# One-bank score buffers for the first four tiles, a buffer of its own for the normalised rows, earlier splits, and weight loads in rows of 512 B

## The chip, the cores and the metric

The kernel runs on one core of a Trainium2 chip. A core has five engines that work side by side and wait for one another through semaphores: TensorE (PE, matmuls; PEld is its weight load), VectorE (DVE), ScalarE (ACT), GpSimd (POOL) and SyncE (SP, which here only issues transfers). Sixteen DMA engines move the data; SP's transfers go over queue q1, those that ACT issues over q10. The metric is the device time of one execution in microseconds (us).

## The reference, cut to what matters

Three stages follow each other. Attention in 4 batches of 8 heads, 576 positions and 64 numbers a head, with a mask by blocks of 64; a two-layer network on the normalised rows; and a choice of one of eight experts for each row.

```
scores = scale * np.matmul(q, k.transpose(0, 1, 3, 2))
scores = np.where(block_i >= block_j, scores, -1000000000.0)
attn = softmax(scores); attn_out = np.matmul(attn, v)          # "a"
x = attn_out.transpose(0, 2, 1, 3).reshape(B, S, H * D)
xn = (x - mu) / np.sqrt(var + 1e-06) * g_ln
x = x + np.maximum(xn @ w_ch1, 0.0) @ w_ch2                    # 512 -> 2048 -> 512
logits = x @ w_gate                                            # then one expert a row
out = p[e] * (np.maximum(x @ w1[e], 0.0) @ w2[e])
```

The inputs are of 64-bit floating point where the two weight matrices w_ch1 and w_ch2 are concerned.

## The kernel before, in words

The 2304 rows are 18 tiles of 128. Tile by tile and head by head the kernel makes scores (qk, L308), their maxima (maxes, L328), exponentials (exps, L339 to L355: exp, rounding to 16 bit, the rest by subtraction, and a transpose by DMA), and the product with v (pv, L370 and L374). Each factor is held as two 16-bit parts, so that a product is three matmuls. `finish` (L392) divides, computes mean and variance of a row (L408 and L409), normalises it (L418), splits it (L422, L423) and has it transposed (L427); L436 to L455 make the row's exact scale out of the variance. The first layer of the network (l1, L473 to L478) and the second (l2, L495 to L497, `post` from L501) work on groups of one to three tiles. `post` splits the new row (L505, L507), writes it (L509) and transposes it (L513), and `logits` (L520 to L525) multiplies it with the gate's weights.

The weights w_ch1 and w_ch2 come as 64-bit numbers, in 32 chunks of 128 x 512. `load_w` brings a chunk as 1024 words of 32 bit a partition into one of three buffers (WB = 3); 3 loads are issued on SP, 29 on ACT. `w_bits` makes 32-bit floats of it on DVE in three steps (L195, L199, L202), `w_hi` (L215, L216 on ACT) and `w_lo` (L220 on POOL) the two parts. Chunks 0 to 15 are w_ch1, 16 to 31 w_ch2; a piece of l2 can run when its four chunks are there.

A tile's k, q and v are split into two parts by `split_k`, `split_q` and `split_v` while the tile before it is at head 3 or 6; the parts of k and q lie in a ring of three buffers with the tag "nat", which the normalised rows (xh, L421) share.

The order on each engine is set when the program is built: a scheduler takes the instructions in the order of the loop from L737 and puts ready ones first by priority. `first(i)` (L720) raises the priority of attention in the first HT tiles; the conversions of weights (WPACE), and the queue of l1 and l2 pieces (L775 to L789) have none. Once built, each engine runs its list in order.

Of the kernel before, what the change touches and what calls it, by code (L numbers as in the profile page):

```python
# [10 lines left out]
F16 = mybir.dt.float16  # L11
# [57 lines left out]
ACAP = 20000  # L69
FREE = 16  # L70
HP = 400
HT = 2
MAN = 0
FS = 7
G2 = 68
# [11 lines left out]
def kernel(  # L87
# [42 lines left out]
    actx = dctx.enter_context(ExitStack())  # L130
    at = actx.enter_context(tc.tile_pool(name="at", bufs=1))
    ps_a = actx.enter_context(tc.tile_pool(name="ps_a", bufs=1, space=PSUM))
    wctx = {"c": ExitStack()}
    wctx["p"] = wctx["c"].enter_context(tc.tile_pool(name="ws", bufs=1))

# [36 lines left out]
        raw[nm, i] = t  # L172

    def load_w(p, eng):
        t = wctx["p"].tile([P, 1024], I32, tag="wraw", name="wraw", bufs=WB)
        if p < 16:
            j, kk = divmod(p, KD)
            src = w_ch1[kk * P:(kk + 1) * P, 2 * j * 512:2 * (j + 1) * 512]
        else:
            src = w_ch2[(p - 16) * P:(p - 15) * P, :]  # L180
        eng.dma_start(out=t, in_=src)
        raw["w", p] = t

    wt = {}

    def w_bits(p):
        r = raw.pop(("w", p)).rearrange("p (n t) -> p n t", t=2)
        top, low = r[:, :, 1], r[:, :, 0]  # L190
        if p < 16:
            t = w2h[:, p % 4 * 2:p % 4 * 2 + 2].rearrange("p c e -> p (c e)").bitcast(I32)
        else:
            t = wp.tile([P, 512], I32, tag=("x2h", "x2t")[p % 2], name="wt", bufs=1)
        nc.vector.tensor_scalar(  # L195
            out=t, in0=top, scalar1=3, scalar2=0x3FFFFFFF,
            op0=ALU.logical_shift_left, op1=ALU.bitwise_and,
        )
        nc.vector.scalar_tensor_tensor(  # L199
            out=t, in0=top, scalar=-0x40000000, in1=t, op0=ALU.bitwise_and, op1=ALU.bitwise_or  # L200
        )
        nc.vector.scalar_tensor_tensor(  # L202
            out=t, in0=low, scalar=29, in1=t, op0=ALU.logical_shift_right, op1=ALU.bitwise_or
        )
        wt[p] = t.bitcast(F32)

    def w_parts(p):
        if p < 16:
# [17 lines left out]

    def split_q(i, eng):
        r = raw.pop(("q", i))
        n = at.tile([P, H, 2, D], F16, tag="nat", name="qn", bufs=3)
        nc.scalar.copy(out=n[:, :, 0], in_=r)  # L230
        eng.tensor_tensor(out=n[:, :, 1], in0=r, in1=n[:, :, 0], op=ALU.subtract)
        o = (KRING + VRING + turn_q[0] % 2 * 2) * 1024
        turn_q[0] += 1
        a, b = (
            spare[:, x:x + 1024].rearrange("p (h c) -> p h c", h=H) for x in (o, o + 1024)
        )
        nc.sync.dma_start_transpose(out=a, in_=n.rearrange("p h e d -> p (h e d)"))
        nc.vector.tensor_copy(b[0:D], a[D:P])
        nc.vector.tensor_copy(b[D:P], a[0:D])
        qt[i, 0], qt[i, 1] = a, b  # L240

    def split_k(i, eng):
        r = raw.pop(("k", i))
        n = at.tile([P, H, 2, D], F16, tag="nat", name="kn", bufs=3)
        nc.scalar.copy(out=n[:, :, 0], in_=r)
        eng.tensor_tensor(out=n[:, :, 1], in0=r, in1=n[:, :, 0], op=ALU.subtract)
        nc.sync.dma_start_transpose(
            out=kt[:, i % KRING], in_=n.rearrange("p h e d -> p (h e d)")
        )
# [36 lines left out]
    def qk(i, h):  # L286
        ks = keys(i)
        nk = len(ks)
        lo, n = span(i)
        m = pack(i)  # L290
        if h % m == 0:
            sps[i] = ps_a.tile([P, 1024], F32, tag="s", name="ps_s", bufs=2)
        sp = sps[i][:, h % m * n:]
        for part in range(2):
            for a, b in runs(i):
                o = lo if a == 0 else 0
                kk = ks[a] % KRING
                x, z = h % 4, h // 4
                if ks[a] % 9 == 4:
                    rhs = kt[:, kk].rearrange("p (x t) (z f s) -> p x z f t s", t=2, z=2, f=2)  # L300
                    rhs = rhs[:, x, z, 1] if o else rhs[:, x, z]
                else:
                    rhs = kt[:, kk:kk + b - a].rearrange(
                        "p n (x t) (z s) -> p x z n t s", t=2, z=2
                    )[:, x, z]
                    if b == a + 1:
                        rhs = rhs[:, 0]
                nc.tensor.matmul(  # L308
                    sp[:, a * P + o:b * P],
                    lhsT=qt[i, part].rearrange("p (x t) c -> p x (t c)", t=2)[:, x, z::2],  # L310
                    rhs=rhs,
                    start=part == 0 and a % 4 == 0,
                    stop=part == 1 and (b == 4 or b == nk),
                )
        sps[i, h] = sp
# [76 lines left out]
    def finish(i):  # L392
        sv = sums.pop(i)
        r = at.tile([P, H], F32, tag="rinv", name="rinv", bufs=2)
        nc.vector.tensor_scalar(
            out=r, in0=sv[:, 1], scalar1=P_S * 1e-9, scalar2=V_S, op0=ALU.add, op1=ALU.mult
        )
        nc.vector.reciprocal(out=r, in_=r)
        ob = obs.pop(i)
        x = wp.tile([P, H, D], F32, tag="x", name="x", bufs=6)  # L400
        nc.gpsimd.tensor_tensor(
            out=x, in0=ob, in1=r[:, :, None].to_broadcast([P, H, D]), op=ALU.mult
        )
        x = x.rearrange("p h d -> p (h d)")
        xt[i] = x
        sm = at.tile([P, 12], F32, tag="lns", name="lns", bufs=2)
        mean, var, y, w = (sm[:, c:c + 1] for c in (6, 7, 8, 9))
        nc.vector.bn_stats(out=sm[:, 0:6], in_=x)  # L408
        nc.vector.bn_aggr(out=sm[:, 6:8], in_=sm[:, 0:6])  # L409
        nc.vector.tensor_scalar(out=var, in0=var, scalar1=LN_EPS, scalar2=None, op0=ALU.add)  # L410


        nc.vector.tensor_scalar(
            out=y.bitcast(I32), in0=var.bitcast(I32), scalar1=-0.5, scalar2=1597463007.0,
            op0=ALU.mult, op1=ALU.add,
        )
        xn = at.tile([P, DM], F32, tag="ob", name="xn", bufs=2)
        nc.vector.tensor_scalar(  # L418
            out=xn, in0=x, scalar1=mean, scalar2=y, op0=ALU.subtract, op1=ALU.mult
        )  # L420
        xh = at.tile([P, 2, DM], F16, tag="nat", name="xh", bufs=3)  # L421
        nc.scalar.copy(out=xh[:, 0], in_=xn)  # L422
        nc.gpsimd.tensor_tensor(out=xh[:, 1], in0=xn, in1=xh[:, 0], op=ALU.subtract)  # L423
        g, j, n = group_of(i)
        if j == 0:
            xg[g] = wp.tile([P, 2 * KD, n * P], F16, tag="xg", name="xg", bufs=2)
        nc.sync.dma_start_transpose(  # L427
            out=xg[g][:, :, j * P:(j + 1) * P], in_=xh.rearrange("p e d -> p (e d)")
        )
        if i in GROUPS[-1]:  # L430
            c = GROUPS[-1].index(i)
            nc.vector.tensor_copy(stats[:, c, 0:1], mean)
            nc.vector.reciprocal(out=stats[:, c, 1:2], in_=y)

        f = fac[:, i:i + 1]
        nc.vector.scalar_tensor_tensor(  # L436
            out=w, in0=y, scalar=var, in1=y, op0=ALU.mult, op1=ALU.mult
        )
        nc.vector.tensor_scalar(
            out=f, in0=w, scalar1=-1.0, scalar2=3.0, op0=ALU.mult, op1=ALU.add  # L440
        )
        nc.vector.scalar_tensor_tensor(
            out=y, in0=f, scalar=w, in1=f, op0=ALU.mult, op1=ALU.mult
        )
        nc.vector.scalar_tensor_tensor(
            out=f, in0=y, scalar=12.0, in1=f, op0=ALU.subtract, op1=ALU.mult
        )
        nc.vector.scalar_tensor_tensor(
            out=y, in0=f, scalar=w, in1=f, op0=ALU.mult, op1=ALU.mult
        )  # L450
        nc.vector.tensor_scalar(
            out=y, in0=y, scalar1=HOUT / 8192.0, scalar2=HOUT * -3.0 / 32.0,
            op0=ALU.mult, op1=ALU.add,
        )
        nc.vector.tensor_tensor(out=f, in0=f, in1=y, op=ALU.mult)  # L455
# [281 lines left out]
    for s in range(nsteps + LAG + MPT):  # L737
# [8 lines left out]
        if s < nsteps:  # L746
            i, h = steps[s]
            with first(i):
                if s + 1 < nsteps:
                    qk(*steps[s + 1])  # L750
                maxes(i, h)
                exps(i, h)
# [2 lines left out]
                load_tile(1)  # L755
            if t + 1 < NTILE:
                nx = ORDER[t + 1]
                if h == SK:
                    split_k(nx, nc.gpsimd)
                if h == SQ:  # L760
                    split_q(nx, nc.gpsimd)
                if h == SV:
                    split_v(nx)
                if h == SL:
                    load_tile(t + 2)
        if s == 24:
# [588 lines left out]
```

## Time and profile before

| | |
|---|---|
| median of 3 runs | 838.18 us (834.8 to 842.07) |
| profiled execution | 843.15 us, span 841.4 us |
| TensorE clock granted, mean | 0.978 |
| PE, DVE, ACT, POOL busy | 707.7, 460.1, 362.1, 327.8 us |
| q1: packets, MB, share of 16 engines | 321472, 100.73, 63.0% |
| q10: packets, MB, share of 16 engines | 4176, 15.21, 6.8% |

The span goes from the first to the last instruction; the 1.75 us beside it are start and end of the execution. An engine's busy time is the sum over its instructions. A row of the timeline gives start, duration, engine, line of the kernel and names, and in brackets how long the engine had been idle and what ended that.

### The profile page before, as it was taken

Reading aid. Unit: us, or ns where it says so; the run is one execution under the profiler, and the core shown is the slowest. Engines: PE = TensorE matmul, PEld = TensorE weight load, DVE = VectorE, ACT = ScalarE, POOL = GpSimd, SP = SyncE. Lnnn points to the kernel's source line nnn. Section 1 sums busy time; section 2 is a strip of 40 time slices with the busy share of each in tenths; the row PEclk is TensorE's granted clock in tenths of the full one; section 3 lists DMA queues with packets and bytes.
Section 4 is the critical chain, followed back from the end, with each engine's and each line's share of the span. In section 5 each row is a group of like instructions: output and inputs, shape, how many; then the busy total and the mean of one; then the engine's idle time right before and its main releaser. Section 6 shows DMA issues by size and latency. Waiting matters only on the chain. (4 is left out here: it accounts for less than half of the span.)

```text
span 841.4 us, 16461 instructions
## 1 busy us (share of the span) xinstructions
PE 707.7 (84%) x5526; PEld 425.4 (51%) x5526; DVE 460.1 (55%) x1248; ACT 362.1 (43%) x843; POOL 327.8 (39%) x364
## 2 busy tenths in 40 slices
PE   0214758789899999898998999998997999999995
PEld 0113645486756857655654565555452444444442
DVE  2999979887755556765564575276881111111110
ACT  2764657675555437555553464164041111111110
POOL 1577747776465235454444553210002122112210
PEclk9999989999999999999999999999998999999999
DMA  9998998799987677799967865397116655665673
GB/s 193 194 227 203 210 203 196 147 184 178 168 144 157 132 141 153 123 184 173 166 131 132 170 100 102 65 341 253 40 43 127 112 125 126 125 121 130 132 129 73
DMA packets 328942, 127.33 MB, mean 151 GB/s; under 512 B 296912, under 2 KB 315344, under 8 KB 328848
## 3 DMA queue, kind: packets, MB, share of 16 engines
q1 hardware_dynamic: 321472, 100.73, 63.0%
q10 hardware_dynamic: 4176, 15.21, 6.8%
q0 software_dynamic: 3200, 10.23, 3.7%
q8 instruction: 48, 0.79, 0.4%
q14 instruction: 46, 0.38, 0.2%
HBM read 128.73 MB, written 9.70 MB: 165 GB/s over the span
## 5 line engine op out<-in xcount | busy, mean ns | idle before, releaser
L473 PE MATMUL dps<-xg,wide 128*128 128x128 f16 (+2 forms) x576 | 156.4, 282 | 28.0 <-DVE htl L478 14.8
L351 POOL TENSOR_TENSOR ph<-sm,ph 128x512 f16<-128x512 f32 (+6 forms) x120 | 132.2, 1105 | 121.8 <-ACT ph L348 83.9
L474 PE MATMUL dps<-xg,wide 128*128 128x128 f16 (+2 forms) x576 | 156.7, 282 | 0.0
L475 PE MATMUL dps<-xg,wide 128*128 128x128 f16 (+2 forms) x576 | 156.6, 282 | 0.0
L339 ACT ACTIVATE sm<-sm,sums 128x128 f32<-128x128 f32 (+8 forms) x144 | 87.9, 611 | 111.5 <-DVE sums L332 100.7
L308 PE MATMUL ps_s<-wide 128*128 128x128 f16 (+4 forms) x560 | 74.9, 260 | 49.2 <-DVE sums L328 27.4
L1001 DVE SCALAR_TENSOR_TENSOR hth<-hps,hth 128x512 f16<-128x512 f32 x38 | 26.2, 691 | 164.6 <-ACT hth L1000 164.4
L495 PE MATMUL dps<-wide,hth 128*128 128x512 f16 x288 | 110.8, 386 | 0.2 <-DVE early L564 0.2
L496 PE MATMUL dps<-wide,hth 128*128 128x512 f16 x288 | 110.7, 385 | 0.0
L497 PE MATMUL dps<-wide,htl 128*128 128x512 f16 x288 | 110.4, 383 | 0.0
L370 PE MATMUL ps_o<-wide,pt 128*128 128x128 f16 x464 | 59.3, 225 | 29.3 <-DVE ob L383 19.0
L474 PEld LDWEIGHTS <-wide 128*128 128x128 f16 x576 | 58.9, 102 | 47.1 <-issue 33.8
L478 DVE SCALAR_TENSOR_TENSOR htl<-dps,hth 128x128 f16<-128x128 f32 (+2 forms) x144 | 59.1, 417 | 42.2 <-ACT hth L477 41.7
L1025 POOL DMA_INDIRECT out<-eo,dst_i x19 | 19.2, 1013 | 156.1 <-ACT eo L1024 151.4
L328 DVE CUSTOM_DVE_ANT_0 sm<-ps_s,mask_a 128x256 f32<-128x256 f32 (+7 forms) x128 | 64.2, 516 | 18.2 <-POOL ph L351 9.6
L308 PEld LDWEIGHTS <-wide 128*128 128x128 f16 x560 | 39.6, 101 | 61.8 <-issue 27.3
L348 ACT CAST ph<-sm 128x512 f16<-128x512 f32 (+6 forms) x120 | 68.2, 570 | 1.6
L477 ACT ACTIVATE hth<-dps 128x128 f16<-128x128 f32 (+2 forms) x144 | 53.5, 375 | 33.5 <-PE dps L475 33.3
L475 PEld LDWEIGHTS <-wide 128*128 128x128 f16 x576 | 59.1, 103 | 14.8
L473 PEld LDWEIGHTS <-wide 128*128 128x128 f16 x576 | 59.1, 103 | 14.6 <-issue 0.6
L370 PEld LDWEIGHTS <-pt 128*128 128x128 f16 x464 | 43.7, 100 | 26.3 <-DMA pt<-ph 17.9
L374 PE MATMUL ps_o<-wide,pt 128*128 128x64 f16 x464 | 55.9, 197 | 0.0
(255 smaller groups left out, 1408.4 us busy)
## 6 DMA issues: line engine op xcount, KB each, us to landing
raws<-in_moe_w SPq DMA_DIRECT2D x38, 2048.0 KB
wraw<-in_moe_w_ch ACTq DMA_DIRECT2D x29, 512.0 KB
raws<-in_moe_w SPq DMA_DIRECT2D x24, 512.0 KB
rows<-x2h SPq DMA_DIRECT2D x18, 256.0 KB
raw<-in_k SPq DMA_DIRECT2D x32, 128.0 KB
raw<-in_q SPq DMA_DIRECT2D x32, 128.0 KB
raw<-in_v SPq DMA_DIRECT2D x32, 128.0 KB
pt<-ph SPq DMA_TRANSPOSE x120
```

The costliest lines, as they stand in the source:

```text
L308: nc.tensor.matmul(sp[:, a * P + o:b * P], lhsT=qt[i, part].rearrange("p (x t) c -> p x (t c)", t=2)[:, x, z::2], rhs=rhs, start=part == 0 ...
L328: nc.vector.tensor_tensor_reduce(out=sm[:, lo:n], in0=sp[:, lo:n], in1=mask[:, 5 * P - n + lo:5 * P], scale=-0.125, scalar=3.0e38, op0=ALU ...
L339: nc.scalar.activation(out=e, in_=e, func=AF.Exp, scale=-1.0, bias=sv[:, 0, h:h + 1], accum_out=sv[:, 1, h:h + 1],)
L348: nc.scalar.copy(out=ph4[:, :, 0, lo:], in_=sm[:, :, lo:])
L351: nc.gpsimd.tensor_tensor(out=ph4[:, :, 1, lo:], in0=sm[:, :, lo:], in1=ph4[:, :, 0, lo:], op=ALU.subtract)
L370: nc.tensor.matmul(o, lhsT=t[:, c], rhs=vt[kk][:, h].rearrange("p e d -> p (e d)"), start=c == 0, stop=False,)
L473: nc.tensor.matmul(hp, lhsT=wh, rhs=xg[g][:, kk], start=kk == 0, stop=False)
L474: nc.tensor.matmul(hp, lhsT=wh, rhs=xg[g][:, KD + kk], start=False, stop=False)
L475: nc.tensor.matmul(hp, lhsT=wl, rhs=xg[g][:, kk], start=False, stop=kk == KD - 1)
L495: nc.tensor.matmul(op[j], lhsT=hh, rhs=w2h[:, f], start=f == 0, stop=False)
L496: nc.tensor.matmul(op[j], lhsT=hh, rhs=w2l[:, f], start=False, stop=False)
L497: nc.tensor.matmul(op[j], lhsT=hl, rhs=w2h[:, f], start=False, stop=f == KF - 1)
```

## The change

Four edits. The score tiles of the first four tiles (FEW) come from a pool of their own, in four buffers of 512 columns (one bank) in place of two of 1024; before tile 4 that pool is closed, and one with two buffers of 1024 columns is opened in the same space. The normalised rows xh get one buffer of their own, and the ring "nat" has two. `first` holds for four tiles in place of two (HT), and it now also covers the splits of those tiles. A weight chunk is loaded in eight rows of 512 B a partition in place of one of 4 KB, into a tile whose rows are 528 B apart; `w_bits` reads it with one dimension more.

```diff
-HT = 2
+HT = 4
+FEW = 4
...
+    sctx = {"c": ExitStack()}
+    sctx["p"] = sctx["c"].enter_context(tc.tile_pool(name="ps_e", bufs=1, space=PSUM))
...
-        t = wctx["p"].tile([P, 1024], I32, tag="wraw", name="wraw", bufs=WB)
+        t = wctx["p"].tile([P, 8, 132], I32, tag="wraw", name="wraw", bufs=WB)
...
-        eng.dma_start(out=t, in_=src)
-        raw["w", p] = t
+        eng.dma_start(out=t[:, :, 0:128], in_=src.rearrange("p (a b) -> p a b", a=8))
+        raw["w", p] = t[:, :, 0:128]
...
-        r = raw.pop(("w", p)).rearrange("p (n t) -> p n t", t=2)
-        top, low = r[:, :, 1], r[:, :, 0]
+        r = raw.pop(("w", p)).rearrange("p a (n t) -> p a n t", t=2)
+        top, low = r[:, :, :, 1], r[:, :, :, 0]
...
+        wt[p] = t.bitcast(F32)
+        t = t.rearrange("p (a n) -> p a n", a=8)
...
-        n = at.tile([P, H, 2, D], F16, tag="nat", name="qn", bufs=3)
+        n = at.tile([P, H, 2, D], F16, tag="nat", name="qn", bufs=2)
...
-        n = at.tile([P, H, 2, D], F16, tag="nat", name="kn", bufs=3)
+        n = at.tile([P, H, 2, D], F16, tag="nat", name="kn", bufs=2)
...
-            sps[i] = ps_a.tile([P, 1024], F32, tag="s", name="ps_s", bufs=2)
+            n = 1024 if i >= FEW else 512
+            sps[i] = sctx["p"].tile([P, n], F32, tag="s", name="ps_s", bufs=2048 // n)
...
-        xh = at.tile([P, 2, DM], F16, tag="nat", name="xh", bufs=3)
+        xh = at.tile([P, 2, DM], F16, tag="xh", name="xh", bufs=1)
...
+                if steps[s + 1:s + 2] == [(FEW, 0)]:
+                    sctx["c"].close()
+                    sctx["p"] = actx.enter_context(tc.tile_pool(name="ps_s", bufs=1, space=PSUM))
...
-                if h == SK:
-                    split_k(nx, nc.gpsimd)
-                if h == SQ:
-                    split_q(nx, nc.gpsimd)
-                if h == SV:
-                    split_v(nx)
+                with first(nx):
+                    if h == SK:
+                        split_k(nx, nc.gpsimd)
+                    if h == SQ:
+                        split_q(nx, nc.gpsimd)
+                    if h == SV:
+                        split_v(nx)
```

The lines of the changed kernel are 7 to 11 higher at the places below: L202, L206 and L209 are the three conversions (L195, L199, L202 before), L335 is a maximum (L328), L415 to L462 the statistics (L408 to L455), L508 the addition in `post` (L501), L315, L377, L381 the matmuls of qk and pv (L308, L370, L374), L527 the first of the logits (L520).

DVE from the last weight chunk to the addition in `post`, before (mask_m marks the maxima of tile 4):

```order
286 L195 TENSOR_SCALAR wt<-wraw 128x512
...
291 L202 SCALAR_TENSOR_TENSOR wt<-wraw,wt 128x512
292 L398 RECIPROCAL rinv<-rinv 128x8
293 L328 ISA sm,sums<-ps_s,mask_m 128x640
...
296 L328 ISA sm,sums<-ps_s,mask_m 128x640
...
299 L328 ISA sm,sums<-ps_s,mask_m 128x640
...
302 L501 SCALAR_TENSOR_TENSOR x<-dps,fac,x 128x512
```

The same place in the changed kernel:

```order
303 L202 TENSOR_SCALAR wt<-wraw 128x512
...
305 L209 SCALAR_TENSOR_TENSOR wt<-wraw,wt 128x512
306 L415 BN_STATS lns<-x 128x6
307 L335 ISA sm,sums<-ps_s,mask_m 128x640
...
313 L425 TENSOR_SCALAR xn<-x,lns 128x512
...
320 L462 TENSOR_TENSOR fac<-fac,lns 128x1
321 L335 ISA sm,sums<-ps_s,mask_m 128x640
...
324 L508 SCALAR_TENSOR_TENSOR x<-dps,fac,x 128x512 x2
```

Before, three maxima of tile 4 stand ahead of the addition, all behind the last chunk; now six do, four of them ahead of the last chunk, and the statistics of tile 3 (L415 to L462) stand between the chunk and the addition.

PE around the first logits, before (128x64 is part of tile 5's scores, xg the first layer of group 2):

```order
1548 L374 MATMUL ps_o<-wide,pt 128x64
1549 L520 LDWEIGHTS x2t
1550 L520 MATMUL dps<-wg_71,x2t 128x9
...
1574 L473 MATMUL dps<-xg,wide 128x128
```

The same in the changed kernel:

```order
1564 L381 MATMUL ps_o<-wide,pt 128x64
...
1566 L315 MATMUL ps_s<-wide 128x64
...
1580 L315 MATMUL ps_s<-wide 128x128
...
1600 L381 MATMUL ps_o<-wide,pt 128x64
1601 L527 LDWEIGHTS x2t
1602 L527 MATMUL dps<-wg_71,x2t 128x9
```

Sixteen score matmuls of tile 5 and ten value matmuls of tile 4, which stood behind the logits, now stand ahead of them.

## Rows read from the trace of the kernel before

**Rows 1.** The page's first lines: busy us, instructions; busy tenths of 40 slices

```profile
span 841.4 us, 16461 instructions
...
PE 707.7 (84%) x5526; PEld 425.4 (51%) x5526; DVE 460.1 (55%) x1248; ACT 362.1 (43%) x843; POOL 327.8 (39%) x364
...
PE   0214758789899999898998999998997999999995
```

**Rows 2.** Windows: stretch, length, busy us per engine, PE clock, DMA share

```profile
40.00:60.00 20.00, 3.61 (x28) 2.50 (x28) 19.81 (x41) 12.50 (x31) 14.05 (x10) 1.00 1.00 229
100.00:120.00 20.00, 14.19 (x156) 9.76 (x156) 17.96 (x42) 12.66 (x36) 12.25 (x10) 1.00 1.14 180
200.00:300.00 100.00, 91.74 (x932) 69.65 (x931) 62.53 (x194) 52.54 (x139) 47.22 (x62) 0.98 0.80 151
```

**Rows 3.** Timeline around the gate, rows of DVE and of PE

```profile
start us, us, engine line op out<-in xcount [idle before <-releaser]
...
157.41 0.69 DVE L202 SCALAR_TENSOR_TENSOR wt<-wraw,wt 128x512 int32<-128x512 int32 x1
...
162.14 0.75 DVE L501 SCALAR_TENSOR_TENSOR x<-dps,fac,x 128x512 f32<-128x512 f32 x1 [1.12 <-PE dps L497]
...
171.55 0.18 PE L520 MATMUL dps<-wg,x2t 128*128 128x9 f16 x1 [1.77 <-DMA x2t<-x2h]
```

**Rows 4.** Lines by form, DVE, 157 to 177 us: count, busy us, mean ns

```profile
L328 DVE CUSTOM_DVE_ANT_0 sm<-ps_s,mask_m 128x640 f32<-128x640 f32 x8 | 6.5, 813 | 0.3 <-POOL ph L351 0.3
```

**Rows 5.** Windows, 167 to 177 us, the tile lns alone

```profile
167.00:177.00 10.00, 6.25 (x12) 0.83 1.03 213
```

**Rows 6.** Timeline, PE, 174 us

```profile
174.13 0.85 PE L308 MATMUL ps_s<-wide 128*128 128x64 f16 x8
```

**Rows 7.** Waits of PE: 180 to 345 us, then 345 to 590

```profile
PE ps_o L370 <- DVE ob L383: 2.8, 2, 2.6
PE ps_o L370 <- DMA pt<-ph: 2.2, 2, 1.2
...
PE ps_s L308 <- DVE sums L328: 1.8, 2, 1.3
```

**Rows 8.** DMA queues: packets, MB, share of 16 engines, 79.75 to 81.5

```profile
q10 hardware_dynamic: 104, 0.37, 52.8%
q1 hardware_dynamic: 248, 0.11, 22.2%
```

**Rows 9.** Waits of DVE: 20 to 100 us, then 100 to 140

```profile
DVE wide L195 <- DMA wraw<-in_moe_w_ch: 0.6, 2, 0.4
...
DVE wt L195 <- DMA wraw<-in_moe_w_ch: 2.3, 2, 1.3
```

**Rows 10.** Timeline: a load's issue, and the two waits for loads

```profile
31.78 0.33 ACTq L181 DMA_DIRECT2D wraw<-in_moe_w_ch  x1
...
39.23 0.45 DVE L195 TENSOR_SCALAR wide<-wraw 128x512 int32<-128x512 int32 x1 [0.43 <-DMA wraw<-in_moe_w_ch]
...
41.29 1.14 DVE L195 TENSOR_SCALAR wide<-wraw 128x512 int32<-128x512 int32 x1 [0.16 <-DMA wraw<-in_moe_w_ch]
```

**Rows 11.** Timeline, DVE, the start

```profile
6.20 0.69 DVE L199 SCALAR_TENSOR_TENSOR wide<-wraw,wide 128x512 int32<-128x512 int32 x1
6.93 0.69 DVE L202 SCALAR_TENSOR_TENSOR wide<-wraw,wide 128x512 int32<-128x512 int32 x1
...
18.72 0.43 DVE L195 TENSOR_SCALAR wide<-wraw 128x512 int32<-128x512 int32 x1 [9.81 <-DMA wraw<-in_moe_w_ch]
```

**Rows 12.** Lines by form, DVE, 20 to 160 us: the conversions

```profile
L202 DVE SCALAR_TENSOR_TENSOR wide<-wraw,wide 128x512 int32<-128x512 int32 x15 | 16.4, 1093 | 0.1
L202 DVE SCALAR_TENSOR_TENSOR wt<-wraw,wt 128x512 int32<-128x512 int32 x16 | 16.1, 1006 | 0.1
L199 DVE SCALAR_TENSOR_TENSOR wt<-wraw,wt 128x512 int32<-128x512 int32 x16 | 15.6, 978 | 0.2
L199 DVE SCALAR_TENSOR_TENSOR wide<-wraw,wide 128x512 int32<-128x512 int32 x14 | 12.0, 856 | 0.0
```

**Rows 13.** DMA queues, 23.5 to 25.5 us, two transposes alone

```profile
q1 hardware_dynamic: 1056, 0.26, 58.1%
```

More of the change, by code (lines that the diff above doesn't have):

```diff
@@ L204, in w_bits @@
         )
-        wt[p] = t.bitcast(F32)
     def w_parts(p):
```

## The prediction

> **What bounds the kernel now.** Start with the page's first two parts [rows 1]: TensorE (PE) is busy for 707.7 of 841.4 us, and its slices, 21 us each, hold 0 to 8 tenths for the first nine and 9 tenths from the tenth on. The means hide two stages, so the windows come next [rows 2]. From 40 to 60 us VectorE (DVE) works 19.81 of 20 us while PE works 3.61; from 100 to 120 DVE still works 17.96; from 200 to 300 PE works 91.74 of 100 and DVE 62.53. Until about 170 us, then, the kernel runs at the pace of DVE, which turns the weights into floats and takes the score maxima; after that at the pace of PE. All that the change touches lies in the first stage, or runs beside a full PE.
>
> The reader is to see next what hands over from one stage to the other. The gate is a chain of single instructions [rows 3]: DVE ends the last weight chunk (L202, started at 157.41), PE's second layer of tiles 0 and 1 uses it, DVE adds the result to x (L501, 162.14), the row is split and transposed, and at 171.55 PE starts L520, the logits of tile 0. The first layer of group 2, the next big block of PE work, stands behind L520 in PE's order. What moves L520 moves everything after it, because from there PE has hardly any idle time to give.
>
> The sum is made against the profiled execution, 843.15 us (span 841.4 and 1.75 around it); the median of the runs shown is 838.18, 4.97 lower. Differences worked out here are added to the median.
>
> **The gate.** In the order of the changed kernel DVE does all that it did before L501, leaves nothing out, and does more: three more maxima of tile 4 and the whole statistics block of tile 3 (L408 to L455 in old lines), which before came after it. A maximum of that shape takes 813 ns [rows 4], three take 2.4 us. The block's instructions were busy 6.25 us in the trace [rows 5]. That is 8.7 us more DVE work ahead of L501. DVE had waited 1.12 us there for PE [rows 3], which this work fills: L501, and so L520, slips by 7.6 us. PE gains work that it may do while it waits: 16 score matmuls of tile 5 and 10 value matmuls of tile 4 now stand ahead of L520. Eight of the former took 0.85 us [rows 6]; 26 at that pace are 2.8 us. Net at the gate: 7.6 - 2.8 = +4.8 us. Its ends: 0, if DVE reaches this place earlier by as much, and 8.7, if PE's extra work doesn't fit.
>
> Behind the gate the order on DVE and PE is nearly the old one, but attention is now ahead of PE by that block. PE's waits there for attention shrink: 2.8 for L383's sums, 2.2 for the transposed probabilities, 1.8 for maxima [rows 7], 6.8 in all. I take half, -3.4, because the lead is used up with time; ends 0 and -6.8.
>
> **Weight loads in rows of 512 B.** The trace has 512 B rows beside 4 KB ones, so the price is there. Within 79.75 to 81.5 us queue q1 moved 0.11 MB (k and q in 512 B rows, and a few 4 B counts) in 22.2% of 16 engines' 1.75 us, 6.2 us of engine time: 29 ns a row. Queue q10 moved 0.37 MB of weights in 52.8%, 14.8 us: 164 ns for 4 KB [rows 8]. Eight rows of 512 B cost 231 ns, 67 more than one of 4 KB; a load has 8 such rows on each engine, so it takes 0.54 us longer. Who waits: DVE, in order, at L195. In 20 to 140 us it waited for a load four times, 2.9 us in all [rows 9], the first at 39.23 for a load issued at 31.78 [rows 10]; the other loads had landed. Four waits longer by 0.54 us: +2.2 us. Ends: -2.9 (the four waits go) and 31 x 0.54 = 16.7 (each load is waited for in full).
>
> The Trainium skill, "DMA: Bandwidth & Descriptors", section Specifications, gives 512 B as the smallest transfer that runs at line rate; by that the rows would cost nothing and the sum would be 2.2 us lower. The rows disagree: 29 ns for 512 B against 164 / 8 = 20.5.
>
> **The start.** DVE's first long wait, 9.81 us until 18.72, is for the fourth weight load [rows 11], while the first transposes share the engines with it. Shorter rows let the transposes through sooner and the load itself later; DVE waits for both. I take 0; ends -1.4 and +2.2 (four loads by 0.54).
>
> **Edits at nothing.** The three conversions now read 8 runs of 64 words instead of one of 512; the elements stay 512, so 0, ends 0 and one wait more or less as above. The four one-bank score buffers let PE run further ahead of the maxima; PE is idle there anyway (3.61 of 20 us [rows 2]), DVE's total stays, so 0. If PE weren't idle the cover would be gone; that is after 180 us, when the buffers are the old two again. The switch between the pools makes tile 4's first scores, and what PE has queued behind them, wait for tile 3's last maximum; PE was idle for 5.8 of 20 us at 100 to 120 [rows 2], which covers it: 0, and up to one maximum, 0.8, without that cover. Earlier splits and the buffer of their own for the normalised rows move work of ScalarE, GpSimd and the SP queue by a few places; no engine but DVE is full there, and what DVE does earlier it does not do later: 0.
>
> Sum: 4.8 - 3.4 + 2.2 = +3.6 us, 838.2 + 3.6 = 841.8: **842 us**, with a range of its own from 836 to 848. A measurement of this kernel can tell about 1% (8.4 us) from no change, so this is no change.
>
> **Rival A: DVE gets through its stage faster.** The conversions take far longer than alone: L202 1093 and 1006 ns, L199 978 and 856 [rows 12], against 690 when nothing ran beside them [rows 11]. The excess is 15 x 0.40 + 16 x 0.32 + 16 x 0.29 + 14 x 0.17 = 18 us of the stage that sets the gate. GpSimd was busy 14.05 and 12.25 of 20 us meanwhile [rows 2], and its operations change places. If half the collisions go (-9.0) and the weight waits with them (-2.9, and the 2.2 not added), the time is 841.8 - 14.1 = 828 us, range 823 to 833. For it: DVE is full, so each saved microsecond counts. Against it: GpSimd's work is the same, as much of it stands ahead of the gate as before and more, and nothing in the change keeps the two apart.
>
> By the Trainium skill, "SBUF — State Buffer", section Who interferes with whom, a DVE instruction with two SBUF inputs and a GpSimd instruction that reads SBUF take turns, and the later one is blocked for the whole of the other; by this rule any new order is a new draw of collisions, in either direction. The 1093 against 690 ns agree with it.
>
> **Rival B: the loads become the wait (slower).** A 4 KB row of weights goes through an engine as one packet; 512 B rows may alternate with the SP queue's 256 B blocks, which alone take 58.1% of 32 us over 1056 packets, 18 ns each [rows 13]. Then a load grows by 0.54 + 64 x 0.018 = 1.7 us. Place: L195. The point from which it decides: three buffers give a load two conversions' time, at 31 conversions in 137 us some 8.8 us; the load of [rows 10] took 7.4, and 9.1 is over it. Eight loads late by 1.7 us are 13.6, less the 2.2 counted: 841.8 + 11.4 = 853 us, range 848 to 860. For it: the DMA engines are busy for 1.00 and 1.14 of the two early windows [rows 2]. Against it: of 20 to 100 us only the two waits of [rows 10] are left in the table [rows 9], so that from 42 to 100 us no load was waited for.
>
> The Trainium skill, "DMA: Bandwidth & Descriptors", section Queues, rings and completion order, says that an engine goes round its queues packet by packet and that a packet may hold several descriptors; were eight rows one packet, B would not come. No run here shows it yet.
>
> **Rival C: the rows stay 4 KB in effect and the slip is covered:** 838 us, 836 to 840.
>
> **How the numbers follow.** Chances: forecast 0.48, A 0.29, B 0.19, C 0.04. Faster than 829.8: most of A, 0.25. Slower than 846.6: B and the forecast's upper edge, 0.24. Within: 0.51. The range leaves out A's lower half and B's upper: 826 to 853.
>
> **What would show it.** Right: the last conversion of a weight chunk near 160 to 166, the first logits matmul near 176 to 183 and PE empty before it; four to eight waits of conversions for loads, and 29 x 1024, some 30,000, packets on q10. A: the two second-step conversions under 900 ns and the logits before 170. B: L195's waits over 10 us. Wrong altogether, if PE's idle time after 200 us, some 8 of 100, changes by more than 7 us: then the order of the splits matters where I put it at nothing.

## The result and the profile after

The changed kernel takes 844.70 us, median of 20 runs (840.61 to 848.0), the kernel before 838.26 (834.49 to 844.77). The ratio is 1.0058 with an interval of 1.0038 to 1.0078: 4.9 us slower, 3.2 to 6.5. (The ratio is not that of the two medians, which lie 6.4 us apart.) The forecast was 842 with a range of its own from 836 to 848, "no change" by its bound of 1%, and that is what came; how much of it was luck is told below. The profiled execution took 844.69 us, its median.

First the page of the changed kernel, its lines as in [rows 1], then the TensorE clock in tenths and the queue of the weights:

```profile
span 842.1 us, 16473 instructions
...
PE 712.7 (85%) x5526; PEld 427.5 (51%) x5526; DVE 449.9 (53%) x1248; ACT 362.9 (43%) x843; POOL 329.3 (39%) x364
...
PE   0223677979899997998999999998997999999995
...
PEclk9999897989999998999999999999998999999998
...
q10 hardware_dynamic: 30160, 15.21, 7.2%
```

The shape is the old one. DVE did the same instructions in 449.9 us, not 460.1, which looks like a gain and was none (E6). The packets on q10 are the 30,000 expected, for a share of 7.2% against 6.8%.

The windows of [rows 2], in the changed kernel:

```profile
40.00:60.00 20.00, 4.83 (x24) 2.44 (x25) 19.89 (x45) 12.65 (x32) 12.45 (x10) 1.00 1.03 232
100.00:120.00 20.00, 15.35 (x177) 11.70 (x177) 19.85 (x44) 14.84 (x37) 13.51 (x11) 0.91 1.03 232
200.00:300.00 100.00, 94.08 (x935) 70.67 (x933) 53.36 (x182) 51.82 (x133) 48.01 (x61) 1.00 0.86 158
```

DVE is as full as before until the gate. Behind it, PE's gaps have become smaller from 200 to 300 us: 94.08 of 100 us are busy, not 91.74. (From 300 to 345 us it is the other way; see the part on the absorption.)

The gate itself, to be read against [rows 3]. The timeline of the changed kernel, DVE, and then the first logits on PE:

```profile
159.29 1.41 DVE L206 SCALAR_TENSOR_TENSOR wt<-wraw,wt 128x512 int32<-128x512 int32 x1
160.74 1.53 DVE L209 SCALAR_TENSOR_TENSOR wt<-wraw,wt 128x512 int32<-128x512 int32 x1
162.19 0.68 DVE L415 BATCH_NORM_STATS2 lns<-x 128x6 f32<-128x512 f32 x1
162.79 0.80 DVE L335 CUSTOM_DVE_ANT_0 sm<-ps_s,mask_m 128x640 f32<-128x640 f32 x1
...
164.11 1.26 DVE L425 TENSOR_SCALAR xn<-x,lns 128x512 f32<-128x512 f32 x1
165.29 1.36 DVE L443 SCALAR_TENSOR_TENSOR lns<-lns 128x1 f32<-128x1 f32 x1
166.69 0.15 DVE L446 TENSOR_SCALAR fac<-lns 128x1 f32<-128x1 f32 x1
166.87 0.89 DVE L449 SCALAR_TENSOR_TENSOR lns<-fac,lns 128x1 f32<-128x1 f32 x1
167.79 1.08 DVE L452 SCALAR_TENSOR_TENSOR fac<-lns,fac 128x1 f32<-128x1 f32 x1
168.91 1.32 DVE L455 SCALAR_TENSOR_TENSOR lns<-fac,lns 128x1 f32<-128x1 f32 x1
...
170.57 0.82 DVE L335 CUSTOM_DVE_ANT_0 sm<-ps_s,mask_m 128x640 f32<-128x640 f32 x1
...
171.51 1.40 DVE L508 SCALAR_TENSOR_TENSOR x<-dps,fac,x 128x512 f32<-128x512 f32 x2
...
178.02 0.18 PE L527 MATMUL dps<-wg,x2t 128*128 128x9 f16 x1 [1.29 <-DMA x2t<-x2h]
```

The last chunk starts its last step at 160.74 (157.41 before), the addition at 171.51 (162.14), the logits at 178.02 (171.55). Between chunk and addition stands the statistics block of tile 3, and four of its instructions on one number a partition take 0.9 to 1.4 us, where L446, of the same size, takes 0.15.

DVE's waits, 20 to 100 us and then 100 to 163 us, the whole answers (see [rows 9]):

```profile
DVE wide L244 <- DMA wide<-qn: 2.0, 1, 2.0
...
DVE ob L390 <- ACT ob L389: 1.0, 1, 1.0
```

No conversion waits for a load any more. And PE's waits, 180 to 345 us, those of [rows 7] and the two largest:

```profile
PE dps L480 <- DVE sums L339: 5.4, 3, 4.3
PE dps L480 <- DVE htl L485: 4.3, 4, 1.7
...
PE ps_o L377 <- DMA pt<-ph: 1.0, 2, 0.7
...
PE ps_o L377 <- DVE ob L390: 0.3, 1, 0.3
PE ps_s L315 <- DVE sums L335: 0.2, 1, 0.2
```

The attention waits of L377 went from 2.8 and 2.2 to 0.3 and 1.0, but L480's wait for the sums of the maxima is new: before it was 0.7 us in the same window:

```profile
PE dps L473 <- DVE sums L332: 0.7, 2, 0.5
```

The last addition of the second layer shows what is left of the gate's slip at the end of the PE stage, before and after:

```profile
629.03 0.74 DVE L501 SCALAR_TENSOR_TENSOR x<-dps,fac,x 128x512 f32<-128x512 f32 x1
```

```profile
629.97 0.74 DVE L508 SCALAR_TENSOR_TENSOR x<-dps,fac,x 128x512 f32<-128x512 f32 x1
```

Of 6.5 us at the logits 0.9 are left there. So this pair of profiles shows 0.7 us of span (842.1 against 841.4) where the runs show 4.9: the first profile of the kernel before was of an execution 5 us above its median (843.15). Its other two (E5, E12) have the same gate and the last addition at 627.5 and 626.9.

### The profile page after: what moved, and what is told of

Same layout as the page of the kernel before. It is cut to its first block, busy times and chain, and to the rows that moved or that the text cites. A ratio compares the mean times of both kernels' runs of the same rounds, so it can differ in the third digit from the quotient of the medians.

```text
span 842.1 us, 16473 instructions
## 1 busy us (share of the span) xinstructions
PE 712.7 (85%) x5526; PEld 427.5 (51%) x5526; DVE 449.9 (53%) x1248; ACT 362.9 (43%) x843; POOL 329.3 (39%) x364
## 5 line engine op out<-in xcount | busy, mean ns | idle before, releaser
L480 PE MATMUL dps<-xg,wide 128*128 128x128 f16 (+2 forms) x576 | 156.9, 283 | 33.4 <-DVE htl L485 18.1
L315 PE MATMUL ps_s<-wide 128*128 128x128 f16 (+4 forms) x560 | 77.0, 265 | 61.1 <-DVE sums L335 30.2
L335 DVE CUSTOM_DVE_ANT_0 sm<-ps_s,mask_a 128x256 f32<-128x256 f32 (+7 forms) x128 | 64.4, 516 | 26.0 <-PE ps_s L315 20.9
L315 PEld LDWEIGHTS <-wide 128*128 128x128 f16 x560 | 40.0, 103 | 68.7 <-DMA wide<-qn 28.1
L377 PE MATMUL ps_o<-wide,pt 128*128 128x128 f16 x464 | 61.4, 227 | 10.2 <-DVE ob L390 6.1
L480 PEld LDWEIGHTS <-wide 128*128 128x128 f16 x576 | 59.1, 103 | 16.4 <-issue 1.9
L484 ACT ACTIVATE hth<-dps 128x128 f16<-128x128 f32 (+2 forms) x144 | 53.5, 376 | 30.7 <-PE dps L482 30.2
L377 PEld LDWEIGHTS <-pt 128*128 128x128 f16 x464 | 44.8, 102 | 25.3 <-DMA pt<-ph 10.5
L381 PE MATMUL ps_o<-wide,pt 128*128 128x64 f16 x464 | 57.5, 199 | 0.0
```

What stands on the lines that cost most here:

```text
L315: nc.tensor.matmul(sp[:, a * P + o:b * P], lhsT=qt[i, part].rearrange("p (x t) c -> p x (t c)", t=2)[:, x, z::2], rhs=rhs, start=part == 0 ...
L335: nc.vector.tensor_tensor_reduce(out=sm[:, lo:n], in0=sp[:, lo:n], in1=mask[:, 5 * P - n + lo:5 * P], scale=-0.125, scalar=3.0e38, op0=ALU ...
L377: nc.tensor.matmul(o, lhsT=t[:, c], rhs=vt[kk][:, h].rearrange("p e d -> p (e d)"), start=c == 0, stop=False,)
L480: nc.tensor.matmul(hp, lhsT=wh, rhs=xg[g][:, kk], start=kk == 0, stop=False)
```

## The experiments

Theory G: the order at the gate decides, and the buffer of its own for the normalised rows makes that order. Rivals: R, the 512 B rows; S, the score buffers or the precedence. Measured, with logits (first L520) and last addition from each profile; the last column is the execution's time less its span, the median of the kernel's runs:

| kernel | median us | ratio to before | logits us | last addition us | beside the span us |
|---|---|---|---|---|---|
| before (three profiles) | 838.3 to 839.8 | 1 | 171.6, 171.1, 170.8 | 629.0, 627.5, 626.9 | 1.72 |
| changed | 844.70 | 1.0058 [1.0038, 1.0078] | 178.0 | 630.0 | 2.56 |
| E1 own buffer only | 839.39 | 1.0002 [0.9971, 1.0033] | 175.9 | 627.7 | 1.74 |
| E2 own buffer undone | 837.58 | 0.9964 [0.9934, 0.9994] | 163.4 | 623.5 | 1.73 |
| E3 rows only | 839.85 | 0.9999 [0.9967, 1.0031] | 163.8 | 625.8 | 1.69 |
| E4 rows undone | 844.49 | 1.0037 [1.001, 1.0065] | 176.9 | 628.2 | 2.39 |
| E6 own buffer after the gate | 838.61 | 0.999 [0.9969, 1.0011] | 164.9 | 626.2 | 2.01 |
| E7 score buffers undone | 841.91 | 1.0022 [1.0001, 1.0043] | 177.1 | 629.5 | 1.70 |
| E8 precedence undone | 844.71 | 1.0068 [1.0047, 1.0088] | 180.5 | 631.8 | 2.18 |
| E9 no scale for tile 3 | 844.30 | 1.0046 [1.0018, 1.0075] | 175.0 | 626.9 | 2.51 |
| E10 late scale | 843.13 | 1.0046 [1.0026, 1.0066] | 165.2 | 630.5 | 1.71 |
| E11 slip alone | 850.08 | 1.0148 [1.0114, 1.0182] | 185.6 | 636.8 | 1.70 |

**E1, the own buffer alone.**

```diff
-n = at.tile(..., tag="nat", name="qn", bufs=3)      # and kn
+n = at.tile(..., tag="nat", name="qn", bufs=2)
-xh = at.tile([P, 2, DM], F16, tag="nat", name="xh", bufs=3)
+xh = at.tile([P, 2, DM], F16, tag="xh", name="xh", bufs=1)
```

> The kernel before with one edit of the four: the normalised rows get a buffer of their own and the ring of the split k and q has two. Theory G (the loss is the later gate, and the gate is later because this buffer lets tile 3's values and tile 4's maxima go ahead of the addition on VectorE): the program's order has 4 maxima of tile 4 more ahead of the addition, 4 x 0.81 = 3.3 us, and 26 matmuls more ahead of the first logits; the logits start at 173 to 178 us against 171.55, and the time is 840 to 845, above the kernel before by 2 to 6. Rival R (the loss comes from the 512 B rows): 838, like the kernel before, since the rows are 4 KB here. Rival S (it comes from the one-bank score buffers or the precedence): 838.

The gate came as expected, 4.3 to 5.1 us late against the three profiles of before, and the time did not: 1.0002, where G had 840 to 845 and R and S had 838. A slip of this size was gone by the last addition (627.7). So a gate this late need not cost time (the interval allows 2.8 us), and by this run alone R and S would stand; E2 decides against both.

**E2, the own buffer undone** in the changed kernel (E1's edit backwards, the other three edits kept).

> The changed kernel with one edit undone: the normalised rows lie in the ring of the split k and q again, three buffers. Theory G: the order at the gate is the old one (one maximum fewer ahead of the addition), the first logits start at 168 to 173 us, and the time is 834 to 840, like the kernel before or a little under it, because the waits for weight loads go too (2.9 us at most). Rival R: 843 to 846, as the changed kernel. Rival S: 843 to 846.

This is the clearest run. The loss is gone, the interval lies under 1 and apart from the changed kernel's, and the gate is 14.6 us earlier than there. It is also some 5 us earlier than I had written, and 7 to 8 earlier than before (E3 and E5 say why). In E2's profile the addition and the logits stand at:

```profile
154.98 1.40 DVE L508 SCALAR_TENSOR_TENSOR x<-dps,fac,x 128x512 f32<-128x512 f32 x2
...
163.39 0.18 PE L527 MATMUL dps<-wg,x2t 128*128 128x9 f16 x1 [0.65 <-DMA x2t<-x2h]
```

Why a buffer moves the order, by the text of the kernel: in the shared ring of three, the split k and q of the next tile wait until the normalised rows of a tile are transposed, and attention with them. The first maximum of tile 2 starts at 84.2 us before, 82.1 in E2, 81.6 in E3 and 84.0 in E6, where the own buffer comes only later; with the own buffer at 61.0 (changed), 62.1 (E1, no other edit) and 60.4 (E8, precedence as before). So it is the buffer that pulls attention ahead of the weights, not the precedence.

**E3, rows of 512 B alone, and E4, rows of 4 KB in the changed kernel.**

```diff
-t = wctx["p"].tile([P, 1024], I32, tag="wraw", name="wraw", bufs=WB)
-eng.dma_start(out=t, in_=src)
+t = wctx["p"].tile([P, 8, 132], I32, tag="wraw", name="wraw", bufs=WB)
+eng.dma_start(out=t[:, :, 0:128], in_=src.rearrange("p (a b) -> p a b", a=8))
```

> The kernel before with one edit: the weights in rows of 512 B. Theory G with the prediction's price: 0.54 us more a load, the four waits of the conversions for loads grow from 2.9 to 5 us, time 838 to 842. Theory G with the price read from the changed kernel's trace (q10 moved the same bytes in 7.2 instead of 6.8 per cent of the engines' time, 0.12 us more a load): no more waits than before, 836 to 839. Rival R: 843 to 846 with conversions that take longer. Rival S: 838.

> The changed kernel with one edit undone: a chunk of weights is one row of 4 KB a partition again. Theory G: 843 to 846 and the first logits at 176 to 180, since the gate's order is that of the changed kernel; waits of conversions for loads under 1 us if they went because the conversions stand later, 2 to 3 us if they went because of the short rows. Rival R: 837 to 840. Rival S: 843 to 846.

Neither moved in time: E3 is at 0.9999, E4 overlaps the changed kernel. E3's waits for loads are two, 0.9 us in all; E4's one, 0.3. R, the rows as the cause of the loss, falls. What short rows cost shows in the queue's share, 7.2% in the changed kernel and 6.4% in E4, but 7.0% in E5 with 4 KB rows: under 1% of 16 engines' time either way.

**E5 and E12, the kernel before again.**

> The kernel before once more, for a second profile of it. Its first profile came from an execution of 843.15 us, 3 to 5 us over the median of its runs, with the first logits at 171.55 us; the kernels of E2 and E3 have nearly its order and had them at 163.4 and 163.8. If the first profile was a late draw of collisions, the logits start near 163 to 167 here, the span is 834 to 838, and the changed kernel's gate is later by 11 to 15 us and not by 6.4. If the 512 B rows are what brought the gate forward in E2 and E3, they start near 171 again.

> The kernel before a third time. Two profiles of it had the first logits at 171.6 and 171.1 us with spans of 841.4 and 839.6; the mean span of its runs is 838.2. If the gate is fixed by the order, it is at 171 again, and the spread of the runs arises behind it; if it has a second value, it is near 164.

In all three profiles the gate is at the same place: 171.6, 171.1 and 170.8. E12's row, and then E3's:

```profile
170.84 0.19 PE L520 MATMUL dps<-wg,x2t 128*128 128x9 f16 x1 [1.38 <-DMA x2t<-x2h]
```

```profile
163.76 0.19 PE L521 MATMUL dps<-wg,x2t 128*128 128x9 f16 x1 [3.44 <-DMA x2t<-x2h]
```

So the first profile was no late draw, and of E5's two readings the second holds: the edit of the rows alone brought the gate forward by 7 us. VectorE was idle for 15.6 us up to the addition in E3, for 22.5 and 20.5 in the first two profiles of before. As this edit also changes DVE's order from the middle of its list on, whether the transfers or the order did it is not separated. The earlier gate brought 1.1 to 3.2 us at the last addition (625.8) and no time that the interval of E3 shows. In the changed kernel the rows did not do it: E4's gate is at 176.9.

The spans of E5 and E12 were 839.6 and 837.4. They differ behind the gate: last addition 627.5 and 626.9, and 212.1 and 210.5 us from there to the end. The windows of 10 us from 20 us behind the last addition, E5 and then E12, have the reason for the second difference:

```profile
647.49:657.49 10.00, 9.95 (x39) 4.21 (x39) 1.38 (x2) 1.19 (x2) 0.00 (x0) 0.83 0.63 88
646.91:656.91 10.00, 9.98 (x47) 4.55 (x47) 1.38 (x2) 1.19 (x2) 0.00 (x0) 1.00 0.81 121
```

In E5 TensorE's granted clock fell to half (0.50 from 649 to 651 us, 1.2 of 2.4 GHz), after PE had been idle for 2.2 us and had started again at 647.54; in these 10 us it did 39 matmuls and not 47. In E12 PE was idle for the same 2.2 us and the clock stayed. Seven of the fourteen profiles have this drop (212.1 to 212.4 us from the last addition to the end; before, E5, the changed kernel, E4, E7, E9, E10), seven have not (210.3 to 210.7). It comes and goes within one kernel, so it is part of the spread and not of the change.

**E6, the own buffer from tile 4 on.**

```diff
+if i < 4:
+    xh = at.tile([P, 2, DM], F16, tag="nat", name="xh", bufs=3)
+else:
+    xh = wctx["late"].tile([P, 2, DM], F16, tag="xh", name="xh", bufs=1)
```

> The kernel of E2 with the buffer of its own for the normalised rows from tile 4 on; tiles 0 to 3 use the ring of the split k and q. Theory G with two effects of the own buffer, a loss at the gate and a gain after it: the gate is that of E2, the logits start at 161 to 168 us; after the gate VectorE's scale instructions of 128x1 no longer stand beside GpSimd's splits of k and q, so that L452 and L455 of the changed kernel take 0.3 to 0.6 us in the mean and not 0.9, and PE is idle for 22 to 25 us and not 27 from the logits to the last addition; the time is 832 to 836. Rival: the collisions are off the path, the time is that of E2, 836 to 839.

The collisions fell and the time did not. DVE from 165 to 560 us (busy us, mean ns of one), E2 and then E6, the same two instructions of the block:

```profile
L455 DVE SCALAR_TENSOR_TENSOR lns<-fac,lns 128x1 f32<-128x1 f32 x15 | 13.6, 905 | 0.4
L452 DVE SCALAR_TENSOR_TENSOR fac<-lns,fac 128x1 f32<-128x1 f32 x15 | 10.6, 705 | 0.4
```

```profile
L458 DVE SCALAR_TENSOR_TENSOR lns<-fac,lns 128x1 f32<-128x1 f32 x15 | 6.2, 414 | 0.4
L455 DVE SCALAR_TENSOR_TENSOR fac<-lns,fac 128x1 f32<-128x1 f32 x15 | 5.3, 356 | 0.3
```

12.7 us less in two lines, and 838.61 against E2's 837.58. My second effect, a gain of the own buffer after the gate through fewer collisions, is not seen. PE's idle time from the logits to the last addition, for which I had written 22 to 25 us, was 29.7, against 27.2 in E2. The plain reading is that in the PE stage DVE's time is off the path; as E6 moves other work too, this is not shown.

**E7 and E8, score buffers and precedence undone** (two buffers of 1024 columns for all tiles; HT = 2).

> The changed kernel with the score buffers undone: two of two banks for all tiles. The own buffer alone (E1) cost nothing and all four edits cost 5 to 6 us, so some other edit joins it. If the order at the gate decides (VectorE has the same set of instructions ahead of the addition as in the changed kernel, with tile 3's statistics), 842 to 846. If the one-bank buffers are the partner, 838 to 841.

> The changed kernel with the precedence of two tiles again. The order at the gate has tile 3's statistics ahead of the addition here too, and 4 maxima instead of 3: if that order decides, 842 to 846. If the precedence of four tiles is the partner of the own buffer, 838 to 841.

Both orders have tile 3's statistics ahead of the addition, and both lose, as G has it. E8 is as slow as the changed kernel: undoing the precedence took nothing off the loss. E7 lost less, 0.22%; its executions (840.98 to 843.84) lie in the lower half of the changed kernel's. That the one-bank buffers are a partner of the own buffer is likely and not shown, as the intervals touch.

**E9, tile 3's exact scale left out** (a constant in its place; nothing else in the order of any engine changes).

```diff
+if i == 3:
+    nc.vector.tensor_scalar(out=f, in0=var, scalar1=0.0, scalar2=HOUT, op0=ALU.mult, op1=ALU.add)
+    return
```

> The changed kernel, with the exact scale of tile 3 left out: one constant is written in place of the seven instructions L443 to L462, so that VectorE does less ahead of the addition, 1.36 + 0.15 + 0.89 + 1.08 + 1.32 + 0.15 + 0.16 = 5.1 us less 0.15, while the order of all else stays on each engine. The addition should start at 166 to 167 us and the first logits at 172.5 to 174 (178.0 in the changed kernel). If the slip at the gate passes to the end in full, 839 to 840.5; if a third of it does, as the line through the ten profiles has it (the last addition moves 0.33 us for each 1 of the first logits), 842.5 to 844; if the gate is not the cause, 844 to 846.

The timeline of E9 at the addition, the logits and the last addition:

```profile
165.79 1.41 DVE L513 SCALAR_TENSOR_TENSOR x<-dps,fac,x 128x512 f32<-128x512 f32 x2 [1.54 <-PE dps L509]
...
175.00 0.19 PE L532 MATMUL dps<-wg,x2t 128*128 128x9 f16 x1 [1.20 <-DMA x2t<-x2h]
...
626.87 0.74 DVE L513 SCALAR_TENSOR_TENSOR x<-dps,fac,x 128x512 f32<-128x512 f32 x1
```

The addition moved 5.7 us, more than the 5.1 taken out, and then waited 1.54 us for PE: the block had hidden PE's second layer. The logits gained 3.0 us, the last addition 3.1 in this pair of profiles; but E9's profile is of an execution of 841.71 us, 2.6 below its median. The median, 844.30, is hardly under the changed kernel's 844.70, and by itself it fits "the gate is not the cause". The interval, 1.0018 to 1.0075, holds both the changed kernel's 1.0058 and the 1.0022 that all of the 3.0 us would give. So E9 decides nothing: what it takes out of the slip is too little to be measured.

**E10, the scale block at the second layer,** in E2's kernel. Here the early logits of the last group read the scale before it is made, so some rows may go to other experts.

```diff
+def scale(i):                      # L446 to L462, called where l2 opens a tile's sum
```

> The kernel of E2 with the scale instructions of 128x1 emitted at a tile's second layer and not in its statistics. They leave the stretch in which GpSimd splits k and q, where they took 0.68 us in the mean. If those collisions cost time after the gate, 833 to 836; if they are off the path, as E6 has it, 836.5 to 839, as E2.

Slower than both readings had it, 843.13, though the gate is near E2's (165.2). PE is idle 30.7 us between logits and last addition, 27.2 in E2. With the rows that may have moved, the run says no more than that this place for the block is worse.

**E11, nine more additions at the gate,** in the kernel before.

```diff
+for _ in range(9 if i == 0 else 0):
+    nc.vector.scalar_tensor_tensor(out=x, in0=o, scalar=0.0, in1=x, op0=ALU.mult, op1=ALU.add)
```

> The kernel before with nine additions of 0 times the second layer's result ahead of the first addition: 9 x 0.75 = 6.7 us more on VectorE at the gate and no other edit. The scheduler answers by putting 100 matmuls of attention more ahead of the first logits. Logits at 177 to 179. If a slip passes in full, 845 to 847; if a third of it does, 841 to 843; if the matmuls put ahead make up for it, 839 to 840.

The logits came at 185.62, 14.4 us late and not 6.7, as maxima slipped in between the additions and the matmuls ahead of the logits wait for them. The last addition is 9.0 us late (mean of before 627.8), the time 1.0148 of before, 12 us, more than any of the three outcomes written down. A late gate can cost time, and here most of the slip came through. It is not a slip alone, though: as expected, 100 matmuls of attention moved ahead of the logits with it, and other work of DVE among the additions.

## Why the prediction was right, step by step

**The gate, +4.8: right in mechanism, too small.** The logits slipped by 6.5 us, 6.8 against the mean of three profiles of before. DVE's part was put at 7.6 and was 9.4. Busy time of DVE up to the addition, counted without overlaps, grew from 139.6 to 153.6 us, and idle time fell by 4.6. The order's set was 8.7 of the 14.0. The rest is mostly the conversions, which I had left as they were: 77.6 us before and 83.0 after in their six rows. The first below answers to the second of [rows 12]; the other two are the first step, L195 before:

```profile
L209 DVE SCALAR_TENSOR_TENSOR wt<-wraw,wt 128x512 int32<-128x512 int32 x16 | 17.7, 1106 | 0.1
...
L202 DVE TENSOR_SCALAR wt<-wraw 128x512 int32<-128x512 int32 x16 | 12.0, 752 | 0.0
L202 DVE TENSOR_SCALAR wide<-wraw 128x512 int32<-128x512 int32 x13 | 9.5, 734 | 0.0
```

This was rival A's mechanism with the other sign: collisions with GpSimd were drawn anew, and the first step, which had more often escaped them (537 and 633 ns in the mean), got them. The traces bear that out: from 20 to 165 us no first step that ran without a TENSOR_TENSOR of GpSimd beside it took over 0.43 us in either profile, and the others took 0.65 in the mean before and 1.05 after. PE's gain of 2.8 us came as 2.9: from addition to logits 9.41 us before, 6.51 after. That it hit so well is one profile's luck: E4, with the same set ahead of its addition, took 7.85.

**The absorption, -3.4: too small, and not by the path that I gave.** In the pair of profiles 5.5 of the 6.5 us were gone at the last addition, against the mean of before 4.6 of 6.8. The three waits of [rows 7], 6.8 us, came down to 1.5, but L480's new wait for the sums, 5.4, took their place. PE's idle time from logits to last addition fell from 28.2 to 23.9, and the windows show where, before and then after:

```profile
171.55:345.00 173.45, 161.26 (x1676) 121.76 (x1677) 112.02 (x378) 100.12 (x278) 91.01 (x110) 0.98 0.84 154
345.00:626.00 281.00, 264.96 (x2131) 155.09 (x2130) 168.76 (x496) 125.28 (x273) 93.28 (x127) 0.98 0.68 147
```

```profile
178.02:345.00 166.98, 152.89 (x1579) 113.58 (x1580) 93.75 (x350) 92.84 (x262) 86.31 (x105) 0.98 0.86 158
345.00:626.00 281.00, 271.21 (x2185) 160.65 (x2184) 166.22 (x509) 127.86 (x280) 94.50 (x127) 0.98 0.67 144
```

Up to 345 us PE was idle for 12.2 us before and 14.1 after, behind it for 16.0 and 9.8. So the slip was not made up near the gate, where a lead of attention would be used up, but behind 345 us. And it goes with the buffer, not with the late gate: from 345 us to the last addition all six kernels with the own buffer from the start have 9.4 to 11.2 us of idle time, the others 12.2 to 16.7, and E11, with the latest gate of all and no own buffer, has 16.7. (E11 made up 4.5 us before 345.) The own buffer thus does two things: it delays the gate, and it lets PE run with fewer gaps later. E1, where the two cancel, fits this; no run separates them cleanly, as in E6, with the buffer from tile 4 on, PE's idle time grew ahead of 345 us. I had said the prediction was wrong altogether if PE's idle time after 200 us changed by more than 7; it fell by 5.4, from 43.6 to 38.2 us. The order of the splits, for which that was to be the sign, mattered all the same.

**The weight waits, +2.2: wrong, in sign too.** The waits went. The four waits of [rows 9] were themselves a high draw: with rows of 4 KB E5 has one, 0.9 us, and E12 two, 1.5. My sign of being right, four to eight such waits, did not come. The price of a packet, 67 ns more for eight, was read from a stretch in which both queues shared the engines; over the whole span q10 needed 7.2% in place of 6.8% of 16 engines' 842 us, 54 us, or 0.12 us a load where I had 0.54. The rule of the Trainium skill that I set against the row ("DMA: Bandwidth & Descriptors", Specifications: 512 B is enough for line rate) was nearer: E3 at 0.9999 agrees with it. Rival B had no place to begin.

**The start, 0: within the spread.** The wait of [rows 11] ended at 16.65 us in the changed kernel, 18.72 before; but E5 and E12 have 17.43 and 16.88, and E4, with rows of 4 KB, 14.53.

**Edits at nothing: one of them carried everything.** "Earlier splits and the buffer of their own for the normalised rows move work ... by a few places ... 0." The order of the changed kernel, from which I counted the gate, is the work of that buffer: without it (E2) the order at the gate is the old one and the loss gone. The short rows, whose order I also put at nothing, move the gate by 7 us when they stand alone (E3). I counted the sum from the order of all four edits together and so had the gate's direction right, but named no edit; building each edit's order by itself would have shown it.

**Where it was luck.** By the terms as measured the sum is 6.5 - 5.5 and no waits, some +1 us at the last addition (2.2 against the mean of before), where I had +3.6 and the runs have +4.9. Without the +2.2 for waits that never came I would have written 1.4. That 842 lies near the result is due to errors that cancelled; the range and "no change" held.

**What stays open.** Of 4.9 us the profiles place 0.9 to 2.2 at the last addition. Another 0.8 lies beside the span: 2.56 us in the changed kernel's runs (2.51 to 2.61), 1.72 before (1.66 to 1.77). Only kernels with both the own buffer and the one-bank buffers have about 2 us or more there, E4, E6, E8 and E9 among them; E2 with only one and E7 with only the other have 1.7. The changed kernel, E4, E8 and E9 (2.2 us and more) also show 45 packets on the queue q14, which the page calls "instruction", where all others, E6 too, show 46 or 47. What the time is, and whether that packet belongs to it, no view shows. The remaining 2 us or so are spread over executions and were not found: spans averaged 841.8 in the changed kernel, 837.8 to 838.3 before.

So: shown is that the own buffer makes the loss, together with other edits (E2 has no loss without it, E1 none with it alone), and that it reorders the start. From E2 to the changed kernel, one edit, the gate is 14.6 us later, the last addition 6.5. That a late gate can cost time is likely from E11. Not shown is that the gate's slip is all of the loss, which E9 cannot tell, nor which other edit is the partner: undoing the rows (E4) or the precedence (E8) left the loss, undoing the one-bank buffers (E7) left less of it, with intervals that touch.

The kernel with the lowest median is E2: one-bank buffers, precedence and short rows without the own buffer, 837.58 us, 0.9964 [0.9934, 0.9994] of the kernel before. With ten kernels compared, an interval that ends this near to 1 is a weak sign of a gain.

## What to carry to other kernels

A buffer's count is an edit to the order of the whole program: compare the order with each edit undone by itself before costing any of them at nothing. A slip at the gate between two stages is not a slip at the end: here from none (E1) to some two thirds (E11) of it reached the last addition. What becomes of it is read from the idle time of the engine behind, stretch by stretch: here PE won back what it did far behind the gate, and by another effect of the same buffer. And one profile of a kernel whose executions spread by 10 us says little about 5 us; three profiles of the same kernel showed which milestones are fixed and which are not.

## What was not expected of the hardware

DVE instructions on one number a partition, 0.2 us alone, took 0.9 to 1.4 us in the block at 165 to 170 us, and one of them (L455) 0.9 in the mean over 15 tiles of E2, where GpSimd split the rows, k and q back to back beside them. GpSimd in E2's timeline, beside a block from 335.79 to 340.0 us:

```profile
336.60 1.16 POOL L430 TENSOR_TENSOR xh<-xn,xh 128x512 f16<-128x512 f32 x1
337.72 1.15 POOL L252 TENSOR_TENSOR kn<-raw,kn 128x512 f16<-128x512 f32 x1
338.83 1.16 POOL L237 TENSOR_TENSOR qn<-raw,qn 128x512 f16<-128x512 f32 x1
```

That these instructions hold DVE up is read from their place in time, no run took them away alone. But the place in time is telling: from 165 to 560 us of E2 L443, L449, L452 and L455 run 60 times; the 20 with no TENSOR_TENSOR of GpSimd beside them took at most 0.22 us, the other 40 took 0.92 in the mean. Taking 12.7 us of that away bought nothing (E6). The mean granted clock over the runs was 0.958 in the changed kernel and 0.971 before. In the changed kernel's page its low slices lie mostly ahead of the gate (0.8 from 84 to 105 us, 0.7 from 126 to 147), where PE does not set the pace; no view ties time to that.
